# Clustered attention and two expert stages on one core: another order for the first three halves of the attention

## The chip, the cores and the metric

One Trainium2 chip, one of its cores. The metric is the device time in microseconds (us) of one execution. The kernel before took 1049.97 us, the median of three runs (1048.81 to 1053.58). Engines in the rows: PE is TensorE, PEld its weight loads, DVE is VectorE, ACT is ScalarE, POOL is GpSimd, SP is SyncE (SPq its queue of DMA issues).

## The reference

Three parts follow each other. The attention works for each of 2 batches x 8 heads on 768 positions of 64 values; each query and key belongs to the nearest of 16 centroids, and a query sees the keys of its own cluster alone.

```python
q_assign = np.argmax(np.einsum('bhsd,hcd->bhsc', q_n, c_n), axis=-1)
k_assign = np.argmax(np.einsum('bhsd,hcd->bhsc', k_n, c_n), axis=-1)
mask = q_assign[:, :, :, None] == k_assign[:, :, None, :]
scores = np.where(mask, scale * np.matmul(q, k.transpose(0, 1, 3, 2)), -1000000000.0)
attn = np.exp(scores - np.max(scores, axis=-1, keepdims=True))
attn = attn / (np.sum(attn, axis=-1, keepdims=True) + 1e-09)
x = np.matmul(attn, v)                       # then [1536, 512]
g = elu(x @ w_in); x = g @ w_out             # 512 -> 2048 -> 512
for e in range(4):                           # p: domain_probs, rows summing to 1
    out += p[:, e:e + 1] * (np.maximum(x @ w1[e], 0.0) @ w2[e])
```

## The kernel before, in words

Products of full precision are made of single-pass ones: every operand is split into a high and a low part (h and l).

The attention takes the heads in 8 pairs (j). A pair has 12 units of 128 queries (six per head), taken two at a time: a *half* w is two units, six halves to a pair, 48 in all. For each unit the steps are: S (scores, do_S: two products of 384 columns of QA with KA, which hold the parts of q and k, then two of QB with KB), M (row maximum, VectorE), E (exponent and row sum, ScalarE), G and R (reciprocal of the sum), P (scaling, GpSimd). Then for each half: T (three groups of four transposes), C and L (the high and low parts of what was transposed: ScalarE, then VectorE, or both GpSimd for four groups of eighteen), V (products with v), X, Y, Z (out of PSUM and into xT). The cluster mask lies inside the score product: QB's and KB's first 16 rows hold one-hots of the clusters of the queries and of the keys; the keys' are times 2^100, less 2^100, so that a key of another cluster gets a huge negative score.

A pair is prepared beforehand: load (DMA of q, k, v), prep_qk (transposes, then high part on ScalarE and low part on VectorE), prep_stacks (DMAs that put these parts into QA, KA, QB, KB; three of them for each of q or k and head), prep_logits (products with the centroids), prep_argmax (three parts on VectorE: maximum and subtraction, rank by a ramp, one-hot), and the one-hots' way into QB and KB. Later pairs do this inside the halves of the pair ahead of them (Q, by prep()); the first pair does it ahead of everything (lines 510 to 544), with first_onehot (line 294) writing QB and KB directly.

Every engine runs its instructions in the order in which they are written, and the framework adds no order of its own. The order of the halves is a sorted list (line 549): each step has a time AT, half w comes PERIOD = 4.6 later than the one before, and some steps have a SHIFT. Only the order counts, not the times. Ahead of S0, E0 and Q0 of half 0 the list's loop inserts the rest of the argmax, the second head's one-hots, and the query preparation of pair 1. All loads and stack transfers are issued on SyncE's one queue, in order. warm(n) (line 504) makes n transposes of the identity that nobody reads.

The first pair's argmax is made for one group at a time; groups 0 and 1 are the queries of the first and second head, 2 and 3 their keys.

Of the kernel before, what the change touches and what calls it, by code (L numbers as in the profile page):

```python
# [34 lines left out]

POOL_SPLITS = (2, 4, 6, 11)
BIG = float(2.0 ** 100)

# [8 lines left out]
def kernel(  # L47
# [31 lines left out]
    identb = const.tile([128, 128], BF16, name="identb")  # L79
    ramp = const.tile([128, 1, C], F32, name="ramp")  # L80
    cc = const.tile([128, HP, 4 * C], F32R, name="cc")
# [22 lines left out]
    def attention():  # L104
# [145 lines left out]
        def prep_argmax(j, part, g0=0, g1=4):  # L250

            yield
            yield
            n = g1 - g0
            if part == 0 and g0 == 0:
                oh_t[j] = (
                    am_p.tile([128, T, 4, 1], F32, tag="mx", name="mx"),
                    am_p.tile([128, T, 4, C], F32, tag="rk", name="rk"),
                    am_p.tile([128, T, 4, C], BF16, tag="oh", name="oh"),
                )  # L260
            if n == 4:
                L, mx, rk, oh = (x.rearrange("p t g c -> p (t g) c") for x in (L_t[j], *oh_t[j]))
            else:
                L, mx, rk, oh = (x[:, :, g0] for x in (L_t[j], *oh_t[j]))
            top = mx.to_broadcast([128, T * n, C])
            if part == 0:
                dve.tensor_reduce(out=mx, in_=L, axis=AX.X, op=ALU.max)
                eng = dve if j == 0 else pool
                eng.tensor_tensor(out=L, in0=L, in1=top, op=ALU.subtract)
            elif part == 1:  # L270
                dve.scalar_tensor_tensor(
                    out=rk, in0=L, scalar=0.0, in1=ramp.to_broadcast([128, T * n, C]), op0=ALU.is_ge, op1=ALU.mult
                )
                dve.tensor_reduce(out=mx, in_=rk, axis=AX.X, op=ALU.max)
            else:
                dve.tensor_tensor(out=oh, in0=rk, in1=top, op=ALU.is_equal)
# [17 lines left out]
        def first_onehot(r, nm):  # L294

            dst, sc, bi = ((QB[r], 1.0, 0.0), (KB[r], BIG, -BIG))[nm == "k"]
            oh = oh_t[0][2]
            for i in range(2):
                ps = ps_t.tile([C, 3 * 128], BF16, tag="t", name="ohps")
                for t in range(3):  # L300
                    pe.transpose(ps[:, t * 128:(t + 1) * 128], oh[:, 3 * i + t, r + 2 * (nm == "k")], identb)
                o = dst[0:C, i * 384:(i + 1) * 384]
                if i == 0:
                    act.activation(out=o, in_=ps, func=AF.Copy, scale=sc, bias=bi)
                else:
                    dve.tensor_scalar(out=o, in0=ps, scalar1=sc, scalar2=bi, op0=ALU.mult, op1=ALU.add)

# [47 lines left out]

        def do_S(w, i):
            u = HALF * w + i
            j, r, t = u // UP, (u % UP) // T, u % T
            s = (2 * j + r) % NSET
            ps = ps_s.tile([128, 2, 512], F32, tag="s", name="s")  # L360
            c = slice(t * 128, (t + 1) * 128)
            for n in range(2):
                m = slice(384 * n, 384 * n + 384)
                pe.matmul(ps[:, n, 0:384], lhsT=QA[s][:, c], rhs=KA[s][:, m], start=True, stop=False)  # L364
            for n in range(2):
                m = slice(384 * n, 384 * n + 384)
                pe.matmul(ps[:, n, 0:384], lhsT=QB[s][:, c], rhs=KB[s][:, m], start=False, stop=True)  # L367
            s_t[u] = ps

# [134 lines left out]
        def warm(n):  # L504

            ps = ps_t.tile([128, 3, 128], F32, tag="t", name="warm")
            for i in range(n):
                pe.transpose(ps[:, i % 3, :], ident, ident)

# [6 lines left out]
        for c in range(C):  # L516
            dve.memset(ramp[..., c:c + 1], float(C - c))
        for i in range(NSET):
# [15 lines left out]
        run(prep_logits(0, "q", 1))  # L534
        for nm in "qk":
            load(1, nm)
        for nm in "qk":
            prep_stacks(0, nm, 1)
        run(*(prep_logits(0, "k", i) for i in range(2)))
        warm(14)  # L540
        run(*(prep_argmax(0, i, g, g + 1) for i in range(3) for g in (0, 2)))
        first_onehot(0, "k")
        first_onehot(0, "q")
        run(prep_v(0, 0))
# [3 lines left out]

        items = sorted(
            (at + PERIOD * w + SHIFT.get((nm, w % (2 * NH)), 0) + (4 if nm[0] == "Q" and w == 0 else 0), w, nm)  # L550
            for nm, at in AT.items() for w in range(NW)
        )
        for at, w, nm in items:
            if w == 0 and nm == "S0":
                run(*(prep_argmax(0, i, g, g + 1) for i in range(3) for g in (1, 3)))
            if w == 0 and nm == "E0":
                first_onehot(1, "q")
                first_onehot(1, "k")
                oh_t.pop(0)
            if w == 0 and nm == "Q0":  # L560
                run(*(prep_qk(1, "q", i) for i in range(2)))
                prep_stacks(1, "q", 0)
            do[nm[0]](w, int(nm[1:]))
# [491 lines left out]
```

## Time and profile before

| | |
|---|---|
| median of 3 runs | 1049.97 us |
| profiled execution | 1049.63 us, span 1047.9 us |
| busy share of the span | PE 98%, PEld 88%, DVE 70%, ACT 50%, POOL 37% |
| instructions | 16446 |
| attention ends (last product with v, L441) | near 248.7 us |

The profile's first part gives each engine's busy share over the whole span; it mixes the attention, in which all engines work, with the two expert stages behind it, in which TensorE works almost alone. A stage is therefore read from windows: the busy time of each engine in a stretch, beside the clock that TensorE was granted (1.00 is 2.4 GHz, 0.50 is 1.2 GHz). The timeline lists the instructions of an engine with start and length; a bracket behind one names what ended the idle time ahead of it. TensorE's instructions are pipelined, so that a length includes time in which the next one already runs.

### The profile page before, as it was taken

How to read it: one execution, taken by the hardware profiler on the slowest of the kernel's cores; microseconds unless marked ns; L12 is line 12 of the kernel's file. 1: busy time of each engine (PE TensorE's matmuls, PEld its weight loads, DVE VectorE, ACT ScalarE, POOL GpSimd, SP SyncE). 2: the span in 40 equal slices, each digit the busy share in tenths (PEclk: the TensorE clock that was granted, in tenths of full speed). 3: DMA queues.
4: the chain of work that ended last, by engine and by line, in shares of the span. 5: the costliest groups of instructions: out<-in, count | busy, mean ns of one | idle time of the engine just before them, and what ended most of it. 6: DMA issues, size and time to landing. Idle time of an engine off the chain costs nothing.

```text
span 1047.9 us, 16446 instructions
## 1 busy us (share of the span) xinstructions
PE 1029.1 (98%) x6253; PEld 918.4 (88%) x6253; DVE 735.4 (70%) x1248; ACT 524.2 (50%) x1081; POOL 392.8 (37%) x394
## 2 busy tenths in 40 slices
PE   8999999999999999999999999999999999999998
PEld 7989999989877888888888898999999898989897
DVE  6999989998689674326576765666666767666665
ACT  4989999988676563324442332233332333332331
POOL 2888888889578766344641000000000000000000
PEclk8999999999999999999999999999999999999999
DMA  8746664431323221010002101111101111001003
GB/s 184 186 109 155 144 145 104 111 92 33 114 96 122 81 96 66 1 41 0 1 1 81 41 1 41 41 41 41 35 7 41 41 42 41 17 25 41 1 1 121
DMA packets 61790, 67.53 MB, mean 64 GB/s; under 512 B 29008, under 2 KB 47440, under 8 KB 61712
## 3 DMA queue, kind: packets, MB, share of 16 engines
q1 hardware_dynamic: 61712, 66.49, 22.4%
q8 instruction: 49, 0.80, 0.3%
q14 instruction: 29, 0.24, 0.1%
HBM read 43.08 MB, written 3.15 MB: 44 GB/s over the span
## 4 chain that ended last, share of the span: by engine, by line
PE 84%; DVE 8%; ACT 4%; issue 2%; DMA 1%; SPq 1%; POOL 1%; DVEq 0%; ACTq 0%; POOLq 0%
PE a L915 35%; PE h L765 23%; PE h L745 10%; PE x L441 5%; PE tps L412 4%; PE s L364 2%; PE s L367 2%; DVE pl L433 2%; DVE nm L373 1%; PE lps L239 1%; PE lps L240 1%; DVE wa L710 1%; ACT ph L425 1%; PE qkps L199 1%; ACT e L382 1%
## 5 line engine op out<-in xcount | busy, mean ns | idle before, releaser
L765 PEld LDWEIGHTS h<-x,w1op 128*128 128x128 f32 x2016 | 257.4, 190 | 10.3 <-ACT r L776 1.2
L765 PE MATMUL h<-x,w1op 128*128 128x256 f32 x2016 | 261.2, 285 | 1.0 <-ACT r L776 1.0
L915 PE MATMUL a<-w2op,gh 128*128 128x512 f32 x768 | 238.4, 392 | 0.0
L915 PEld LDWEIGHTS a<-w2op,gh 128*128 128x128 f32 x768 | 138.0, 188 | 23.9
L924 DVE SCALAR_TENSOR_TENSOR acc<-a,prob,acc 128x512 f32<-128x512 f32 x180 | 129.7, 746 | 40.2 <-PE a L915 40.2
L915 PE MATMUL a<-w2op,gl 128*128 128x512 f32 x384 | 149.8, 390 | 0.0
L745 PE MATMUL h<-xT,wh 128*128 128x512 f32 x384 | 118.5, 390 | 0.6 <-DVE gg L754 0.5
L400 POOL TENSOR_SCALAR p<-e,sm 128x768 f32<-128x768 f32 x96 | 88.4, 927 | 40.2 <-DVE sm L394 29.0
L754 DVE SCALAR_TENSOR_TENSOR gg<-r,h 128x512 f32<-128x512 f32 x48 | 32.9, 685 | 96.5 <-ACT r L753 75.4
L373 DVE TENSOR_REDUCE nm<-s 128x1 f32<-128x768 f32 x96 | 90.9, 947 | 2.8 <-PE s L367 2.6
L382 ACT ACTIVATE e<-s,nm 128x768 f32<-128x768 f32 x96 | 86.6, 902 | 4.5 <-POOL p L400 2.8
L412 PE MATMUL tps<-ident,p 128*128 128x128 f32 x576 | 83.5, 277 | 2.9 <-DVE pl L433 2.7
L745 PEld LDWEIGHTS h<-xT,wh 128*128 128x128 f32 x384 | 71.9, 188 | 16.2 <-DVE gg L754 1.4
L776 ACT ACTIVATE r<-h 128x256 f32<-128x256 f32 x48 | 18.4, 384 | 134.8 <-PE h L765 134.8
L915 PEld LDWEIGHTS a<-w2op,gl 128*128 128x128 f32 x384 | 72.1, 188 | 15.6
L433 DVE TENSOR_TENSOR pl<-tps,ph 128x512 fp32r<-128x512 f32 x112 | 76.2, 683 | 6.6 <-ACT ph L425 5.2
L441 PE MATMUL x<-ph,v 128*128 128x256 f32 x288 | 76.6, 298 | 1.4 <-DVE xs L461 1.3
L752 ACT ACTIVATE r<-h 128x512 f32<-128x512 f32 x48 | 28.6, 595 | 97.7 <-PE h L745 96.9
L915 PE MATMUL a<-gh,wh 128*128 128x512 f32 x192 | 74.9, 390 | 1.0 <-ACT acc L931 0.9
L755 POOL TENSOR_SCALAR gh<-gg 128x512 fp32r<-128x512 f32 x48 | 41.0, 854 | 92.0 <-DVE gg L754 89.2
L915 PE MATMUL a<-gl,wh 128*128 128x512 f32 x192 | 74.8, 390 | 0.0
L915 PE MATMUL a<-gh,wl 128*128 128x512 f32 x192 | 74.7, 389 | 0.0
(152 smaller groups left out, 1942.1 us busy)
## 6 DMA issues: line engine op xcount, KB each, us to landing
st<-in_moe_w_dram SPq DMA_DIRECT2D x32, 512.0 KB, 4.3
st<-in_moe_w_in_dram SPq DMA_DIRECT2D x14, 512.0 KB, 3.7
st<-in_moe_w_out_dram SPq DMA_DIRECT2D x14, 512.0 KB, 4.6
QA<-qh SPq DMA_DIRECT2D x32, 192.0 KB, 4.2
nq<-in_q_dram SPq DMA_DIRECT2D x16, 192.0 KB, 3.8
nk<-in_k_dram SPq DMA_DIRECT2D x16, 192.0 KB, 3.9
nv<-in_v_dram SPq DMA_DIRECT2D x8, 384.0 KB, 3.9
QB<-ql SPq DMA_DIRECT2D x16, 192.0 KB, 4.2
```

The lines of the kernel that those rows point to most:

```text
L373: dve.tensor_reduce(out=m_t[w][:, i:i + 1], in_=s_t[HALF * w + i][:, :, 0:384], axis=AX.XY, op=ALU.max, negate=True)
L382: act.activation(out=e, in_=s_t.pop(u)[:, :, 0:384], func=AF.Exp, bias=m_t[w][:, i:i + 1], accum_out=e_t[w][0][:, i:i + 1])
L400: pool.tensor_scalar(p, e_t[w][1 + i].rearrange("p a b -> p (a b)"), e_t[w][0][:, i:i + 1], 1.0, ALU.mult, ALU.mult)
L412: pe.transpose(ps[:, x, :], p_t[w][i][:, c * 128:(c + 1) * 128], ident)
L433: dve.tensor_tensor(out=l, in0=ps, in1=h.bitcast(F32), op=ALU.subtract)
L441: pe.matmul(x_t[w], lhsT=v2[j][:, r, c, :], rhs=t[:, :, c, :], start=(c == 0 and t is ph[w]), stop=(c == T - 1 and t is pl[w]),)
L745: pe.matmul(ps, lhsT=w[:, 0, f], rhs=x, start=(kk == 0 and i == 0), stop=(kk == KD - 1 and i == 2))
L754: dve.scalar_tensor_tensor(out=gg, in0=r, scalar=-1.0, in1=ps, op0=ALU.add, op1=ALU.max)
L755: pool.tensor_scalar(gh, gg, 1.0, 0.0, ALU.mult, ALU.add)
L765: pe.matmul(ps, lhsT=w[wz][kk], rhs=x[xz][:, kk], start=(start and kk + i == 0), stop=(stop and kk == 1 and i == 2), skip_group_check=True,)
L915: pe.matmul(ps, lhsT=x, rhs=y, start=(opens and i == 0), stop=(closes and i == len(ops) - 1))
L924: dve.scalar_tensor_tensor(out=t, in0=ps, scalar=pr, in1=t, op0=ALU.mult, op1=ALU.add)
```

## The change

For the first pair, the query clusters of both heads are found first, in one argmax over two groups (ramp is doubled for it), then the first head's keys, then the second head's. A one-hot is transposed into one PSUM tile; queries are copied by ScalarE alone, keys half by ScalarE and half by VectorE. A score can be written in two parts, QA x KA (do_SA) and QB x KB (do_SB); the first two scores have their first parts ahead of the keys' one-hots. The load of the next pair's keys stands behind the second head's stack transfers in place of ahead of them. The identity transposes are 25, 3, 4 and 6 ahead of the list, and four times 4 in it (54 in place of 39), in a PSUM tile of V's pool. Halves 0, 1 and 2 are placed by a start and a pace of their own (0.6, 0.8, 0.9 of AT); W and Q steps keep their places. From the third transpose group of half 4 on, the order of the list is the one of before.

```diff
--- before.py
+++ after.py
@@ -34,6 +34,8 @@
 }
 
 POOL_SPLITS = (2, 4, 6, 11)
+
+WARM = ((2.65, 4), (4.8, 4), (5.6, 4), (6.6, 4))
 BIG = float(2.0 ** 100)
 
 
@@ -77,7 +79,7 @@
     const = ctx.enter_context(tc.tile_pool(name="const", bufs=1))
     ident = const.tile([128, 128], F32, name="ident")
     identb = const.tile([128, 128], BF16, name="identb")
-    ramp = const.tile([128, 1, C], F32, name="ramp")
+    ramp = const.tile([128, 1, 2 * C], F32, name="ramp")
     cc = const.tile([128, HP, 4 * C], F32R, name="cc")
     prob = const.tile([128, B * T, E], F32, name="prob")
 
@@ -260,16 +262,23 @@
                 )
             if n == 4:
                 L, mx, rk, oh = (x.rearrange("p t g c -> p (t g) c") for x in (L_t[j], *oh_t[j]))
+            elif n == 1:
+                L, mx, rk, oh = (x[:, :, g0] for x in (L_t[j], *oh_t[j]))
             else:
-                L, mx, rk, oh = (x[:, :, g0] for x in (L_t[j], *oh_t[j]))
-            top = mx.to_broadcast([128, T * n, C])
+                L, mx, rk, oh = (x[:, :, g0:g1] for x in (L_t[j], *oh_t[j]))
+            shape = [128, T, n, C] if 1 < n < 4 else [128, T * n, C]
+            top = mx.to_broadcast(shape)
             if part == 0:
                 dve.tensor_reduce(out=mx, in_=L, axis=AX.X, op=ALU.max)
                 eng = dve if j == 0 else pool
                 eng.tensor_tensor(out=L, in0=L, in1=top, op=ALU.subtract)
             elif part == 1:
+                both = len(shape) == 4
+                x, y = (z.rearrange("p t g c -> p t (g c)") if both else z for z in (L, rk))
+                order = ramp if both else ramp[..., 0:C]
                 dve.scalar_tensor_tensor(
-                    out=rk, in0=L, scalar=0.0, in1=ramp.to_broadcast([128, T * n, C]), op0=ALU.is_ge, op1=ALU.mult
+                    out=y, in0=x, scalar=0.0, in1=order.to_broadcast([128, x.shape[1], order.shape[2]]),
+                    op0=ALU.is_ge, op1=ALU.mult,
                 )
                 dve.tensor_reduce(out=mx, in_=rk, axis=AX.X, op=ALU.max)
             else:
@@ -295,15 +304,15 @@
 
             dst, sc, bi = ((QB[r], 1.0, 0.0), (KB[r], BIG, -BIG))[nm == "k"]
             oh = oh_t[0][2]
-            for i in range(2):
-                ps = ps_t.tile([C, 3 * 128], BF16, tag="t", name="ohps")
-                for t in range(3):
-                    pe.transpose(ps[:, t * 128:(t + 1) * 128], oh[:, 3 * i + t, r + 2 * (nm == "k")], identb)
-                o = dst[0:C, i * 384:(i + 1) * 384]
-                if i == 0:
-                    act.activation(out=o, in_=ps, func=AF.Copy, scale=sc, bias=bi)
-                else:
-                    dve.tensor_scalar(out=o, in0=ps, scalar1=sc, scalar2=bi, op0=ALU.mult, op1=ALU.add)
+            ps = ps_t.tile([C, S], BF16, tag="t", name="ohps")
+            for t in range(T):
+                pe.transpose(ps[:, t * 128:(t + 1) * 128], oh[:, t, r + 2 * (nm == "k")], identb)
+            if nm == "q":
+                act.activation(out=dst[0:C], in_=ps, func=AF.Copy)
+                return
+            a, b = slice(0, 384), slice(384, 768)
+            act.activation(out=dst[0:C, a], in_=ps[:, a], func=AF.Copy, scale=sc, bias=bi)
+            dve.tensor_scalar(out=dst[0:C, b], in0=ps[:, b], scalar1=sc, scalar2=bi, op0=ALU.mult, op1=ALU.add)
 
         def run(*gens):
             for g in gens:
@@ -354,18 +363,29 @@
         s_t, m_t, e_t, p_t, ph, pl, t_t, x_t, xs_t, q_t = ({} for _ in range(10))
 
         def do_S(w, i):
+            do_SA(w, i)
+            do_SB(w, i)
+
+        def do_SA(w, i):
             u = HALF * w + i
+            if u in s_t:
+                return
             j, r, t = u // UP, (u % UP) // T, u % T
             s = (2 * j + r) % NSET
-            ps = ps_s.tile([128, 2, 512], F32, tag="s", name="s")
+            ps = s_t[u] = ps_s.tile([128, 2, 512], F32, tag="s", name="s")
             c = slice(t * 128, (t + 1) * 128)
             for n in range(2):
                 m = slice(384 * n, 384 * n + 384)
                 pe.matmul(ps[:, n, 0:384], lhsT=QA[s][:, c], rhs=KA[s][:, m], start=True, stop=False)
+
+        def do_SB(w, i):
+            u = HALF * w + i
+            j, r, t = u // UP, (u % UP) // T, u % T
+            s = (2 * j + r) % NSET
+            c = slice(t * 128, (t + 1) * 128)
             for n in range(2):
                 m = slice(384 * n, 384 * n + 384)
-                pe.matmul(ps[:, n, 0:384], lhsT=QB[s][:, c], rhs=KB[s][:, m], start=False, stop=True)
-            s_t[u] = ps
+                pe.matmul(s_t[u][:, n, 0:384], lhsT=QB[s][:, c], rhs=KB[s][:, m], start=False, stop=True)
 
         def do_M(w, i):
             if i == 0:
@@ -503,9 +523,9 @@
 
         def warm(n):
 
-            ps = ps_t.tile([128, 3, 128], F32, tag="t", name="warm")
+            ps = ps_x.tile([128, 2, 128], F32, tag="x", name="warm")
             for i in range(n):
-                pe.transpose(ps[:, i % 3, :], ident, ident)
+                pe.transpose(ps[:, i % 2, :], ident, ident)
 
         c0, cn = load_centroids()
         load(0, "q")
@@ -514,7 +534,7 @@
         pool.tensor_copy(identb, ident)
         warm(25)
         for c in range(C):
-            dve.memset(ramp[..., c:c + 1], float(C - c))
+            dve.memset(ramp[..., c::C], float(C - c))
         for i in range(NSET):
             for t in (QB[i], KB[i]):
                 pool.memset(t[0:32].bitcast(F32), 0.0)
@@ -532,34 +552,54 @@
         run(*(prep_qk(0, "k", i) for i in range(2)))
         prep_stacks(0, "k", 0)
         run(prep_logits(0, "q", 1))
-        for nm in "qk":
-            load(1, nm)
+        load(1, "q")
         for nm in "qk":
             prep_stacks(0, nm, 1)
-        run(*(prep_logits(0, "k", i) for i in range(2)))
-        warm(14)
-        run(*(prep_argmax(0, i, g, g + 1) for i in range(3) for g in (0, 2)))
+        load(1, "k")
+        run(prep_argmax(0, 0, 0, 2))
+        run(prep_logits(0, "k", 0))
+        run(prep_argmax(0, 1, 0, 2), prep_argmax(0, 2, 0, 2))
+        run(prep_logits(0, "k", 1))
+        warm(3)
+        for r in range(2):
+            first_onehot(r, "q")
+        run(*(prep_argmax(0, i, 2, 3) for i in range(3)))
+        for i in range(2):
+            do_SA(0, i)
+        warm(4)
         first_onehot(0, "k")
-        first_onehot(0, "q")
+        run(*(prep_argmax(0, i, 3, 4) for i in range(3)))
+        warm(6)
         run(prep_v(0, 0))
         NW = NPAIR * 2 * NH
         do = dict(S=do_S, M=do_M, E=do_E, G=do_G, R=do_R, P=do_P, T=do_T, C=do_C, L=do_L, V=do_V, X=do_XC, Y=do_XA,
                   Z=do_XS, Q=do_Q, W=do_W)
 
-        items = sorted(
-            (at + PERIOD * w + SHIFT.get((nm, w % (2 * NH)), 0) + (4 if nm[0] == "Q" and w == 0 else 0), w, nm)
-            for nm, at in AT.items() for w in range(NW)
-        )
-        for at, w, nm in items:
-            if w == 0 and nm == "S0":
-                run(*(prep_argmax(0, i, g, g + 1) for i in range(3) for g in (1, 3)))
-            if w == 0 and nm == "E0":
-                first_onehot(1, "q")
+        def place(at, w, nm):
+            if w > 2 or nm[0] in "QW":
+                return at + PERIOD * w + (4 if w == 0 and nm[0] == "Q" else 0)
+            at0, pace = ((1.5, 0.6), (4.6, 0.8), (9.2, 0.9))[w]
+            return at0 + pace * at
+
+        items = [
+            (place(at, w, nm) + SHIFT.get((nm, w % (2 * NH)), 0), w, nm) for nm, at in AT.items() for w in range(NW)
+        ]
+
+        def start(w, i):
+            if i == 0:
                 first_onehot(1, "k")
                 oh_t.pop(0)
-            if w == 0 and nm == "Q0":
-                run(*(prep_qk(1, "q", i) for i in range(2)))
-                prep_stacks(1, "q", 0)
+            elif i < 3:
+                run(prep_qk(1, "q", i - 1))
+                if i == 2:
+                    prep_stacks(1, "q", 0)
+            else:
+                warm(WARM[i - 3][1])
+
+        items += [(at, 0, f"_{i}") for i, at in enumerate((2.6, 2.7, 4.3))]
+        items += [(at, 0, f"_{i + 3}") for i, (at, _) in enumerate(WARM)]
+        do["_"] = start
+        for at, w, nm in sorted(items):
             do[nm[0]](w, int(nm[1:]))
         run(*w_gen)
         actx.close()
```

## Rows read from the trace of the kernel before

**Rows 1.** Windows: length, busy us (instructions) per engine, clock, DMA share, GB/s

```profile
10.00:20.00 10.00, 9.55 (x53) 8.43 (x52) 6.39 (x25) 2.37 (x7) 0.84 (x1) 0.66 1.03 218
20.00:34.00 14.00, 12.48 (x92) 10.90 (x93) 12.77 (x27) 11.67 (x30) 6.97 (x9) 1.00 0.96 221
34.00:50.00 16.00, 15.49 (x123) 14.75 (x122) 15.12 (x26) 15.06 (x36) 14.21 (x17) 1.00 0.72 178
60.00:80.00 20.00, 19.02 (x146) 17.78 (x146) 18.87 (x35) 18.02 (x42) 18.88 (x22) 1.00 0.44 107
```

**Rows 2.** Granted TensorE clock where it fell and rose, same columns

```profile
11.60:11.70 0.10, 0.10 (x3) 0.10 (x2) 0.00 (x0) 0.00 (x0) 0.00 (x0) 0.50 0.56 123
18.40:18.50 0.10, 0.10 (x2) 0.10 (x2) 0.07 (x2) 0.00 (x0) 0.00 (x0) 0.87 1.51 313
```

**Rows 3.** Identity transposes (warm): ns min/median/max, first and last start

```profile
L508 PE MATMUL warm<-ident x7: 421/421/421, 3.1 to 4.4; 128*128 128x128 f32 x7
...
L508 PE MATMUL warm<-ident x11: 272/273/273, 4.8 to 5.9; 128*128 128x128 f32 x11
...
L508 PE MATMUL warm<-ident x14: 421/421/474, 12.9 to 15.7; 128*128 128x128 f32 x14
```

**Rows 4.** Timeline of TensorE: start, length (us), engine, line, operation

```profile
12.92 3.25 PE L508 MATMUL warm<-ident 128*128 128x128 f32 x14
16.10 1.60 PE L301 MATMUL ohps<-identb,oh 128*16 128x128 bf16 x12
17.63 0.97 PE L364 MATMUL s<-KA,QA 128*128 128x384 f32 x2
18.43 0.52 PE L367 MATMUL s<-KB,QB 96*128 96x384 f32 x2
...
20.32 0.67 PE L301 MATMUL ohps<-identb,oh 128*16 128x128 bf16 x9 [0.67 <-DVE oh L276]
...
24.34 0.30 PE L239 MATMUL lps<-cc,qh 128*128 128x64 f32 x1
...
25.03 0.60 PE L364 MATMUL s<-KA,QA 128*128 128x384 f32 x2
```

**Rows 5.** Timeline of VectorE, same columns

```profile
11.25 0.25 DVE L245 TENSOR_TENSOR L<-lps,ltmp 128x96 f32<-128x96 f32 x1
...
13.58 0.24 DVE L267 TENSOR_REDUCE mx<-L 128x6 f32<-128x96 f32 x1
...
15.40 0.42 DVE L276 TENSOR_TENSOR oh<-rk,mx 128x96 bf16<-128x96 f32 x2
17.02 0.55 DVE L306 TENSOR_SCALAR KB<-ohps 16x384 fp32r<-16x384 bf16 x1 [1.21 <-PE ohps L301]
...
20.35 0.95 DVE L373 TENSOR_REDUCE nm<-s 128x1 f32<-128x768 f32 x1
...
24.21 0.95 DVE L373 TENSOR_REDUCE nm<-s 128x1 f32<-128x768 f32 x1
...
29.68 0.69 DVE L433 TENSOR_TENSOR pl<-tps,ph 128x512 fp32r<-128x512 f32 x1 [0.52 <-ACT ph L425]
```

**Rows 6.** Timeline of ScalarE, same columns

```profile
16.69 0.48 ACT L304 ACTIVATE KB<-ohps 16x384 fp32r<-16x384 bf16 x1 [3.32 <-PE ohps L301]
...
21.51 0.88 ACT L382 ACTIVATE e<-s,nm 128x768 f32<-128x768 f32 x1
...
24.92 0.87 ACT L201 ACTIVATE kh<-qkps 128x384 fp32r<-128x384 f32 x2 [0.68 <-DMA KB<-kh]
```

**Rows 7.** Timeline of GpSimd, same columns

```profile
26.64 1.80 POOL L400 TENSOR_SCALAR p<-e,sm 128x768 f32<-128x768 f32 x2 [15.80 <-DVE sm L394]
```

**Rows 8.** Timeline of SyncE's DMA queue, same columns

```profile
14.89 1.29 SPq L146 DMA_DIRECT2D nk<-in_k_dram  x2
...
20.23 1.47 SPq L228 DMA_DIRECT2D KB<-kh  x1
```

**Rows 9.** One DMA issue: KB each, us to landing

```profile
KB<-kh SPq DMA_DIRECT2D x1, 192.0 KB, 4.6
```

## The prediction

> **What bounds the kernel now.** I read the windows by stage first. From 34 to 80 us TensorE is busy 15.49 of 16 and 19.02 of 20 us, and VectorE 15.12 and 18.87 [rows 1]: two engines in lockstep, each with 5% or less to spare, so a lag carried into this stretch can shrink by little and leaves with the rest of the program, whose instruction order from the fifth half of the attention on (its third transpose group) is the same in both kernels. What can change is therefore the start, before some 34 us. There the reader sees VectorE busy 6.39 of 10 us (10 to 20 us) and 12.77 of 14 (20 to 34), and a TensorE clock of 0.66 on average between 10 and 20 us [rows 1]: it falls to 0.50 (1.2 GHz) at 11.6 us, after a run of small logits matmuls with gaps, and is back at 2.4 GHz from 18.45 [rows 2]. Identity transposes are 421 ns long at the low level and 272 at the full one [rows 3]; their spacing is 3.18 / 14 = 0.227 us low [rows 4] and 1.1 / 10 = 0.11 full [rows 3].
>
> Third, the timelines, which give the chain that starts the attention: last logits sum, argmax of two cluster groups on VectorE (13.58 to 15.82), one-hot transposes (16.10), copies (from 16.69), first scores (17.63), the argmax of the two other groups, and the first row maximum M at 20.35 [rows 4 to 6]. From that M on VectorE hardly rests.
>
> **The change part by part.** All times are on the profiled execution's clock: span 1047.9 us, 1049.63 with the 1.73 us around it; the median of the runs is 0.34 above.
>
> *Argmax of the queries together, before the keys.* The query logits are summed by 11.50 [rows 5]. VectorE's step takes 0.25 us for 96 elements and 0.69 for 512 [rows 5], so one of 192 lies between; on the line through both it is 0.35. Five such and the first key half's logits sum (0.25): 11.50 + 1.75 + 0.25 = 13.5 us for both heads' query clusters, 2.3 us sooner than before.
>
> *TensorE from there, at the low clock.* Its work up to 12.92 is as before, so the clock should fall at the same place. Three warm transposes take 0.68 (13.60), twelve query one-hot transposes 1.60 [rows 4] (15.20), the first parts of two scores 2 x 0.80 (17.63 to 18.43 is one) (16.80), four transposes 0.91 (17.70), six key one-hots 0.80 (18.50). The copies KB end 0.60 later (0.55 each, side by side on ScalarE and VectorE) [rows 5, 6]: 19.10. The query copies go to ScalarE whole: between 0.48 and 0.96, I take 0.9, hidden under 16.8 to 18.5. VectorE's argmax of key group 2 (five steps of 0.25 and a gap, 13.58 + 5 x 0.27 = 14.95 [rows 5]) is hidden too. The argmax of group 3 is queued behind the KB copy: 19.10 + 1.35 = 20.45. M follows at 20.5: **+0.15** against 20.35. The second parts of the scores, behind six more transposes, are done near 20.3, in its shadow. Splitting a score costs nothing else: nothing else wants its two buffers then. The sooner queries win nothing, because keys still stand behind them.
>
> *What follows M.* One copy of a query one-hot leaves VectorE after M: **-0.5** (0.55 less overlap). But the order now lets the two engines wait on each other. ScalarE: exponent of unit 0 (until 22.35), KB half (22.8), query half qh (23.2). VectorE: M to 21.45, KB half to 21.95, then ql, which needs qh, and behind it in the queue M of unit 1, whose scores are long there: VectorE stands from 21.95 to 23.25, **1.3**. M then ends at 24.65, the exponent at 25.55, the second qh at 25.95: VectorE stands from 24.65 to 26.0, **1.35**. The next M (third score) starts at 26.45; before it started at 24.21 [rows 5, 6].
>
> *The reordered load.* SyncE's queue issues the next keys at 14.89; now six stack transfers go first, which puts the issue where the last of those was, 20.23 [rows 8], landing 4.6 us on [rows 9]: 24.8. The DMA engines are at 1.03 and 0.96 of capacity with 218 and 221 GB/s [rows 1], so the last of the same sixteen transfers lands when it did. What goes is ScalarE's wait of 0.68 for KB<-kh at 24.92 [rows 6]; what is late next are these keys. TensorE's transposes of them stand ahead of the third score in its queue, and TensorE has nothing from about 22.1 (second query half) to 24.85. The third score then runs at 25.2 to 26.0, just within VectorE's wait for ql: no further term while that cover lasts; without it the wait alone puts the third M at 26.05 instead of 24.21.
>
> *First transposes ahead of the fifth score's M.* The fourth M starts near 28.4. Then TensorE has four warm transposes, logits (24.34 to 25.03, 0.69) [rows 4], four more, the fifth score (two rows like that of 25.03, overlapping: 0.8) and only then the transposes of half 0, done at 31.3; POOL's p is ready sooner (27.5 + 0.9 [rows 7]). ScalarE's copy of 512 elements takes between 0.48 (384) and 0.88 (768) [rows 6], I take 0.6; VectorE's pl follows at 31.9, before the fifth M in the queue. VectorE stands idle from 29.3, less one logits sum of 0.25: **2.35**. Before, pl came at 29.68 [rows 5], but with the fifth M already done.
>
> *More warm transposes*: 54 for 39, in all 15 more, but eleven fewer ahead of the first one-hots; the twelve behind the third score take 12 x 0.11 = 1.3 us of TensorE, which are in the times above.
>
> A rule against the change: the Trainium skill (TensorE: Matmul & The Clock Gate, Part 4: PE-mode transpose) says that transposes do not count as activity that brings the full clock. In the trace they did: with nothing but transposes on TensorE they went from 421 to 272 ns near 4.8 us [rows 3]. But 14 others ran through at 421. By the rule the low clock would last on past 18.45; by the rows it ends as before, which is what I sum with. The rule's own time stands under the rivals.
>
> **Sum.** +0.15 - 0.5 + (1.3 + 1.35 + 2.35 = 5.0) - 1.23 (the waits VectorE had from 20 to 34 us, 14.00 - 12.77 [rows 1], which these replace) = +3.4 at 34 us. In 34 to 50 and 60 to 80 VectorE had 0.88 + 1.13 = 2.0 us idle; with transposes and products of the first halves already done sooner in its order I let half of that be regained: -1.0. Total +2.4: 1049.63 + 2.4 = **1052.0 us**.
>
> **Rivals.**
> *Faster, the waits hidden.* If the clock is back when the first scores start (15.2), their parts take 0.8, the warm transposes 0.44, the one-hots 0.45 [rows 3, 4]: KB at 17.5, argmax at 18.85, M at 18.9, 1.45 us sooner. If besides the two engines don't wait on each other, -1.45 - 0.5 - 1.23 = -3.2: 1046.4. For it: query one-hots and dense scores now fill the stretch where 14 transposes were. Against: keys land at 24.8 whatever the clock, and the queues' orders are plain.
>
> *Nothing.* The 3.4 us are made good by 80 us, or the waits are half as long as I read: 1049.6, plus or minus 1. For it: engines with slack of 5% over 46 us have 2.3 us to give. Against: VectorE and TensorE wait for each other there.
>
> *Clearly slower: the clock falls again.* TensorE idles from 22.1 to 24.85 behind the keys. If the clock falls on that and stays low as long as it did before (11.6 to 18.45, 6.85 us [rows 2]), half of 6.85 is lost where nothing is to spare: 1049.6 + 3.4 + 3.4 = 1056.4. It decides if the granted clock shows 0.50 again between 22 and 32 us. For it: the clock fell at 11.6 although TensorE was busy 9.55 of the 10 us from 10 to 20 [rows 1]. Against: transposes stand on both sides of the gap.
>
> *Transposes that don't hold the clock* (the rule above). The low clock past 18.45: six transposes 1.36 and the score's second part to 20.8, M at 20.85 instead of 20.5: 1052.4. The first 25 transposes of the trace speak against it.
>
> **How the numbers follow.** Forecast 0.45 (1050.5 to 1054), faster with hidden waits 0.27 (1045.5 to 1048.5), nothing 0.13, clock falls 0.10 (1054.5 to 1058), transposes that don't count 0.05. A measurement here can tell 0.5%, 5.2 us, from no change: faster means under 1044.7, slower over 1055.2. No case reaches the first but the tail of the second, 0.03; slower takes most of the clock case and a tail of the forecast, 0.09; the rest, 0.88, is within. Range 1046 to 1056: it reaches to the means of both outer cases, and takes in the logits and argmax bounds (0.25 to 0.69 a step, five steps, at most 1.7 us).
>
> **What would show it.** Right: the clock row falls at 11.6 and rises near 18.4; M near 20.5; the third M near 26.4; VectorE's waits before ql on ScalarE; TensorE idle ahead of the transposes of the next keys, released by a DMA; VectorE idle from 20 to 34 us about 5 us. Wrong: the third M at or before 24.2, or a clock that is back by 15 us, or a VectorE that from 34 to 80 us shows under half its 2.0 us of idle time. The forecast fails if the first three halves' transposes, done sooner, let TensorE reach the common order earlier than before.

## The result, and the profile after

The changed kernel takes 1066.55 us (median of 6 runs, 1063.95 to 1068.71) against 1051.59 for the kernel before: ratio 1.0144, 95% interval 1.0118 to 1.0169. That is 15 us slower, clearly, where 1052.0 and no more than 1056 were forecast. The kernel before varies more than its first three runs showed (1048.81 to 1056.35 over all comparisons), so each ratio below is to its runs beside the kernel told of, on the same chip. Three of the six runs behind 1051.59 are among its quickest (1048.81 to 1049.97), and its medians in the later comparisons are 1053.59 to 1054.47. Against those the loss is 12 to 13 us, so a difference of a few thousandths between 1.0144 and a ratio below is less than it looks. Disturbed executions are left out; for e4 and e5 the profiled one was among them, so that no profile of theirs is used.

All of it is in the attention's start. The row maximum of the first unit of a half starts as follows (us, from the timelines of VectorE):

| half | 0 | 1 | 2 | 3 | 4 | 5 | 6 | 47 |
|---|---|---|---|---|---|---|---|---|
| before | 20.35 | 24.21 | 27.97 | 32.08 | 36.60 | 41.48 | 46.66 | 256.12 |
| after | 19.48 | 26.63 | 37.16 | 44.84 | 50.22 | 57.22 | 64.21 | 274.12 |
| lag | -0.9 | +2.4 | +9.2 | +12.8 | +13.6 | +15.7 | +17.6 | +18.0 |

The lag is made in halves 1 to 6 and then carried to the end nearly unchanged (17.6 and 18.0). It is 18 us and not 15, since the two profiled executions took 1067.57 and 1049.63 us. The windows that answer to those of before [rows 1]:

```profile
10.00:20.00 10.00, 7.79 (x66) 6.18 (x64) 6.80 (x23) 3.59 (x8) 0.69 (x1) 1.00 0.99 217
20.00:34.00 14.00, 9.99 (x54) 9.60 (x52) 6.03 (x11) 5.19 (x13) 1.79 (x2) 0.73 0.89 196
34.00:50.00 16.00, 12.66 (x76) 10.39 (x74) 8.72 (x17) 9.75 (x23) 8.96 (x11) 0.91 0.36 86
60.00:80.00 20.00, 18.58 (x140) 17.45 (x139) 17.40 (x32) 15.96 (x39) 13.14 (x18) 0.98 0.63 148
```

VectorE is busy 6.03 and 8.72 us in the second and third row; before it was 12.77 and 15.12. TensorE's clock is 1.00 from 10 to 20 us, where it had been 0.66, but 0.73 from 20 to 34: it falls later. Near the fall and the rise:

```profile
26.00:27.00 1.00, 1.00 (x8) 0.96 (x7) 0.37 (x1) 0.51 (x2) 0.00 (x0) 0.79 0.71 151
27.00:36.00 9.00, 9.00 (x40) 8.81 (x39) 2.80 (x6) 1.89 (x5) 1.79 (x2) 0.50 0.91 202
36.00:37.00 1.00, 0.73 (x5) 0.33 (x4) 0.61 (x2) 1.00 (x3) 0.00 (x0) 0.59 0.00 0
```

Nine whole microseconds at 1.2 GHz and a part of two more (0.42 and 0.82 by the means): 10.2 us, in the middle of the halves and not ahead of them as before [rows 2]. A second stretch of 3.4 us follows between 57 and 61 us, 0.50 at its bottom:

```profile
57.00:58.00 1.00, 1.00 (x6) 0.86 (x6) 1.00 (x2) 1.00 (x3) 0.00 (x0) 0.65 0.00 0
...
60.00:61.00 1.00, 1.00 (x8) 1.00 (x7) 0.91 (x2) 0.76 (x2) 0.78 (x2) 0.65 0.46 86
```

TensorE's timeline shows what went before the first:

```profile
20.55 0.82 PE L201 MATMUL qkps<-ident,nq 128*128 128x128 f32 x6
25.37 0.52 PE L201 MATMUL qkps<-ident,nk 128*128 128x128 f32 x3 [4.01 <-DMA nk<-in_k_dram]
...
26.43 0.92 PE L528 MATMUL warm<-ident 128*128 128x128 f32 x4
...
30.35 1.05 PE L528 MATMUL warm<-ident 128*128 128x128 f32 x4
...
33.10 0.99 PE L379 MATMUL s<-KA,QA 128*128 128x384 f32 x2
...
34.53 1.91 PE L432 MATMUL tps<-ident,p 128*128 128x128 f32 x8
...
40.78 0.39 PE L461 MATMUL x<-ph,v 128*128 128x256 f32 x1 [0.70 <-POOL ph L450]
42.12 0.39 PE L461 MATMUL x<-pl,v 128*128 128x256 f32 x1 [0.96 <-POOL pl L451]
...
43.86 0.59 PE L379 MATMUL s<-KA,QA 128*128 128x384 f32 x2
```

The next pair's keys arrive 4.01 us after TensorE was ready for them (I had 2.75). The clock then falls within 1.3 us, and from there everything up to the transposes of 34.53 runs at the low clock: the two score products at 33.10 take 0.99 us, the two at 43.86, at the full clock, 0.59. At 40.78 and 42.12 TensorE stands again, now for GpSimd. VectorE's timeline:

```profile
19.48 0.95 DVE L393 TENSOR_REDUCE nm<-s 128x1 f32<-128x768 f32 x1
21.85 0.54 DVE L315 TENSOR_SCALAR KB<-ohps 16x384 fp32r<-16x384 bf16 x1 [1.42 <-ACT KB L314]
...
25.16 0.56 DVE L205 SCALAR_TENSOR_TENSOR ql<-qkps,qh 128x384 fp32r<-128x384 f32 x1 [1.44 <-ACT qh L203]
26.63 0.96 DVE L393 TENSOR_REDUCE nm<-s 128x1 f32<-128x768 f32 x1 [0.91 <-PE s L388]
...
36.39 0.26 DVE L247 TENSOR_TENSOR L<-lps,ltmp 128x96 f32<-128x96 f32 x1 [4.68 <-ACT ltmp L245]
36.56 0.68 DVE L453 TENSOR_TENSOR pl<-tps,ph 128x512 fp32r<-128x512 f32 x1
37.16 0.95 DVE L393 TENSOR_REDUCE nm<-s 128x1 f32<-128x768 f32 x1
...
44.12 0.42 DVE L481 TENSOR_TENSOR xs<-x,xt 64x256 f32<-64x256 f32 x1 [4.02 <-ACT xt L473]
44.84 0.96 DVE L393 TENSOR_REDUCE nm<-s 128x1 f32<-128x768 f32 x1 [0.31 <-PE s L388]
...
54.06 0.42 DVE L481 TENSOR_TENSOR xs<-x,xt 64x256 f32<-64x256 f32 x1 [2.35 <-ACT xt L473]
...
62.98 0.42 DVE L481 TENSOR_TENSOR xs<-x,xt 64x256 f32<-64x256 f32 x1 [2.07 <-ACT xt L473]
```

There are three stretches. First come waits of 1.42 and 1.44 us for ScalarE (forecast 1.3 and 1.35), with 0.91 us more for the third score, which stands behind the late keys in TensorE's queue. Then come 4.68 us until ScalarE has copied the first transposes and, behind them in its queue, the part ltmp of the next pair's logits:

```profile
35.62 0.60 ACT L445 ACTIVATE ph<-tps 128x512 fp32r<-128x512 f32 x1 [6.08 <-PE tps L432]
36.11 0.24 ACT L245 ACTIVATE ltmp<-lps 128x96 f32<-128x96 f32 x1
```

Last come 4.02 us ahead of Y (xs), behind which the fourth half's row maximum (44.84) stands in the queue; ahead of the next two Y it is 2.35 and 2.07 us again, and the lag grows on. The wait at 44.12 leads to GpSimd:

```profile
38.35 1.79 POOL L420 TENSOR_SCALAR p<-e,sm 128x768 f32<-128x768 f32 x2 [8.79 <-DVE sm L414]
40.10 0.62 POOL L450 TENSOR_SCALAR ph<-raw 128x512 fp32r<-128x512 f32 x1
40.81 1.26 POOL L451 TENSOR_TENSOR pl<-raw,ph 128x512 fp32r<-128x512 f32 x1
```

GpSimd scales half 1 first (1.79 us), because that stands first in its queue, then splits the third group of half 0 (0.62 and 1.26). The product with v of half 0 needs that split, and in TensorE's queue it stands ahead of the score of half 3 (43.86).

### The profile page after: what moved, and what is told of

Same layout as the page of the kernel before. It is cut to its first block, busy times and chain, and to the rows that moved or that the text cites. A ratio compares the mean times of both kernels' runs of the same rounds, so it can differ in the third digit from the quotient of the medians.

```text
span 1065.6 us, 16458 instructions
## 1 busy us (share of the span) xinstructions
PE 1036.0 (97%) x6268; PEld 923.3 (87%) x6268; DVE 734.7 (69%) x1241; ACT 525.3 (49%) x1081; POOL 393.0 (37%) x394
## 4 chain that ended last, share of the span: by engine, by line
PE 81%; DVE 7%; POOL 4%; ACT 4%; issue 2%; DMA 1%; SPq 0%; DVEq 0%; POOLq 0%; ACTq 0%
PE a L955 35%; PE h L805 23%; PE h L785 10%; PE x L461 4%; PE tps L432 3%; POOL p L420 2%; PE s L379 2%; PE s L388 2%; DVE pl L453 1%; DVE nm L393 1%; ACT ph L445 1%; PE warm L528 1%; PE qkps L201 1%; DVE wa L750 1%; POOL xT L493 1%
## 5 line engine op out<-in xcount | busy, mean ns | idle before, releaser
L794 DVE SCALAR_TENSOR_TENSOR gg<-r,h 128x512 f32<-128x512 f32 x48 | 32.9, 685 | 96.5 <-ACT r L793 75.0
L432 PEld LDWEIGHTS tps<-ident,p 128*128 128x128 f32 x576 | 65.9, 142 | 10.4 <-DVE pl L453 4.8
```

Source lines behind the costliest of these rows:

```text
L432: pe.transpose(ps[:, x, :], p_t[w][i][:, c * 128:(c + 1) * 128], ident)
L794: dve.scalar_tensor_tensor(out=gg, in0=r, scalar=-1.0, in1=ps, op0=ALU.add, op1=ALU.max)
```

## The experiments

Compared are ratios to the kernel before; the changed kernel has 1.0144. "Theory" and "rival" are those of the expectation that stands above each result.

**e1, keys first.** The next pair's keys loaded ahead of the stacks.

```diff
-        load(1, "q")
+        for nm in "qk":
+            load(1, nm)
         for nm in "qk":
             prep_stacks(0, nm, 1)
-        load(1, "k")
```

> The changed kernel with one part undone: the load of the next pair's keys stands ahead of the second head's stack transfers again, as before the change. Theory (keys and order): the changed kernel is some 15 us slower because TensorE stands 4.0 us for these keys and then runs 9.6 us (26.8 to 36.4) at the low clock, and because the compressed order of the first three halves makes VectorE and TensorE wait for GpSimd afterwards. Then this kernel gets back the 4.0 us, and 4.8 us for half of 9.6: some 1058 us, and the granted clock stays at 1.00 from 20 to 36 us. Rival (the order alone): the wait was covered by the waits between VectorE and ScalarE, and the time stays within 2 us of 1066.5.

1065.22 us, ratio 1.011 (1.0086 to 1.0133). There is no wait for the keys, yet the fifth unit's maximum starts at 37.20 as in the changed kernel (37.16), and the clock is at 0.50 from 28.3 to 45.3 us. (This was the longest of the four executions, 1068.44; the others took 1063.85 to 1066.46.) The rival comes nearer: the late load alone is not it, and the low clock comes without it.

**e2, the old order of the halves,** keys still late.

```diff
-            if w > 2 or nm[0] in "QW":
+            if True:
```

> The changed kernel with one part undone: all halves of the attention are placed as before the change (no pace of their own for the first three), the late load of the keys stays. Theory (keys and order): the wait for the keys and the low clock stay, what the order cost behind them goes (the lag grew from 9.2 us at the third half's row maximum to some 17 at the seventh's): some 1059 us. Rival (keys alone): the order is harmless once the clock is up, and the time stays above 1064.

1053.56 us, ratio 1.0015 (0.9995 to 1.0035). More than the theory gave it: nine tenths of the loss are gone by ratio, 13.0 us by the medians, with a wait of 2.1 us for the keys still in the trace and no low clock behind it.

**e3, the clock held** by 36 transposes in the wait.

```diff
                 if i == 2:
                     prep_stacks(1, "q", 0)
+                    warm(36)
```

> The changed kernel with 36 more identity transposes behind the second half of the next pair's queries, where TensorE waits for the keys (about 4 us of work at 0.11 us each, inside the wait of 4.0 us). It tells the wait from the clock. Theory: the wait stays, the clock stays at 1.00 through 27 to 36 us, and half of the 9.6 us at the low clock comes back: some 1062 us. Rival (the wait itself does the harm, TensorE's clock is covered by other engines): within 2 us of 1066.5. Second rival (transposes do not count for the clock): the clock falls near 27 us all the same.

1063.67 us, ratio 1.0096 (1.0078 to 1.0114). The windows of the transposes and of what was low before:

```profile
22.80:26.80 4.00, 4.00 (x39) 4.00 (x38) 1.90 (x4) 2.37 (x7) 0.00 (x0) 1.00 0.43 96
27.00:36.00 9.00, 8.32 (x66) 7.80 (x63) 5.86 (x13) 5.30 (x15) 2.31 (x3) 1.00 0.93 209
```

The clock is at 1.00 from 20.2 us until it falls at 40.6, for 3.4 us:

```profile
40.00:41.00 1.00, 1.00 (x9) 1.00 (x9) 0.00 (x0) 0.70 (x2) 0.80 (x1) 0.82 0.00 0
...
44.00:45.00 1.00, 0.70 (x4) 0.38 (x2) 1.00 (x3) 0.92 (x3) 0.76 (x1) 0.97 1.03 246
```

What the low clock was worth is told only roughly: 5 us by the ratios (1.0144 less 1.0096), 3 by the medians. Two executions of the changed kernel with the same mean clock as e3's four (0.995) took 1063.95 and 1064.88, hardly more than e3's 1063.30 to 1065.43. Most of the loss is there with the clock held. Its chain of waits between the row maxima of halves 2 and 3 (start, us, what):

```profile
35.26 0.08 DVE sm L414
...
35.50 1.79 POOL p L420 x2
37.29 0.60 POOL ph L450
...
37.96 1.27 POOL pl L451
...
39.27 0.39 PE x L461
...
41.71 0.64 PE s L379 x2
...
43.03 0.96 DVE nm L393
```

Scaling, split, product, score, maximum: one engine after another, at full clock up to the product (39.27); the score behind it runs at the low one.

**e4, keys first and the old order** (both edits above).

> The changed kernel with both undone: keys loaded ahead of the second head's stacks, and all halves placed as before the change. What is left is the joint argmax of the queries, the one-hots in one piece, the first scores in two parts and the identity transposes. Theory (keys and order are all of it): 1048.5 to 1052 us, as before the change, perhaps 1 us under it since the first row maximum comes 0.9 us sooner. Rival (the waits between ScalarE and VectorE around the next pair's query preparation, or the 15 more transposes, cost by themselves): 1054 or more.

1051.77 us, ratio 0.9985 (0.9973 to 0.9997): with what is left of the change the kernel is about 1.6 us quicker on the mean. At the same clock it is not: e4's eight executions with a mean granted clock of 0.996 or more took 1051.14 to 1052.27 us, four such of the kernel before beside them 1049.53 to 1050.56. But of e4's executions only one had a lower clock (0.994, 1053.83), of the kernel before's 14 (0.992 to 0.995, 1053.10 to 1055.21). The late keys cost 2 us (medians) to 3 (ratios) under the old order, e2 against e4; the two intervals touch.

**e5, products late**, and **e6, transposes and products late**, in halves 0 to 2.

```diff
-            if w > 2 or nm[0] in "QW":
+            if w > 2 or nm[0] in "QWVXYZ":     # e5
+            if w > 2 or nm[0] in "QWTCLVXYZ":  # e6
```

> The changed kernel, but in the first three halves the products with v and what follows them (steps V, X, Y, Z) keep the places of before; all other steps stay compressed. With the old order of all steps the kernel took 1053.6 us, so the compressed order costs 13. Theory (the chain through GpSimd): with V, X and Y early, the product of the first half stands in TensorE's queue behind GpSimd's splits, and the fourth half's first row maximum stands in VectorE's queue behind Y: 4.0 us of VectorE idle from 40.1 to 44.1, and once more a half later. Then some 6 of the 13 us come back: 1060. Rival (the transposes do the harm): no change, over 1064.

> The changed kernel, but in the first three halves all steps from the transposes on (T, C, L and V, X, Y, Z) keep the places of before; only scores, maxima, exponents, reciprocals and scaling stay compressed. Theory (transposes and products pulled ahead of the next halves' scores make every engine wait on the slowest): nearly all of the 13 us come back, 1053 to 1056. Rival (the order of maxima and exponents among the preparation does it): 1060 or more.

e5: 1060.53 us, ratio 1.0052 (1.0033 to 1.0071), as expected. e6: 1059.11 us, ratio 1.0044 (1.0023 to 1.0064): between theory and rival, and as a whole not told apart from e5. Among the executions with a mean clock of 0.995 or more, four of each, e6 took 1055.75 to 1056.59 and e5 1057.60 to 1058.77, so the transposes' places are worth some 2 us there. Something else of the compressed order is left: e6's five executions at 0.992 or less took 1061.62 to 1063.98.

**e7, half 0 alone compressed.**

```diff
-            if w > 2 or nm[0] in "QW":
+            if w > 0 or nm[0] in "QW":
```

> The changed kernel, but only the first half has a start and pace of its own; halves 1 and 2 stand as before the change. If the harm is the first half's transposes and products being ahead of the scores of halves 2 and 3 (theory), most of it stays: 1060 or more. If it comes from the three compressed halves running into each other (rival), it falls to 1057 or less.

1056.56 us, ratio 1.003 (1.0016 to 1.0044): the rival. The harm grows with the number of halves that run into each other.

**e8, no transposes in the list** (WARM empty).

> The changed kernel without the four groups of four identity transposes within the list of halves. In the profile 12 of them run at the low clock between 26 and 33 us, some 0.25 us each, ahead of scores. Theory: they cost up to 3 us of TensorE there, and they do not hold the clock: 1063 to 1065. Rival (they keep the low clock shorter): 1068 or more.

1067.73 us, ratio 1.012 (1.0105 to 1.0135): not told apart from the changed kernel. The clock is at 0.50 all the way from 24.2 to 44.6 us, against 10.2 us with them, and the time is not longer. That engines that wait in turn cover much of a low clock is a reading that no run here tests.

**e9, queries later,** and **e10, the same without the list's transposes,** on e4.

```diff
-        items += [(at, 0, f"_{i}") for i, at in enumerate((2.6, 2.7, 4.3))]
+        items += [(at, 0, f"_{i}") for i, at in enumerate((2.6, 4.25, 4.3))]
```

> The changed kernel with the keys loaded ahead of the stacks and all halves placed as before (together 1051.8 us), and besides the next pair's first half of queries prepared behind the second unit's row maximum, together with the second half, not between the two maxima. Theory (VectorE and ScalarE wait for each other there, 1.3 and 1.35 us in the forecast, 1.42 and 1.44 in the changed kernel's trace): 1 to 2.5 us less, 1049.3 to 1050.8, and under the kernel before. Rival (these waits are covered by TensorE's and GpSimd's): no change, 1051.3 to 1052.3.

> The same without the 16 identity transposes in the list of halves. Theory (TensorE is not the bound of that stretch, but 12 of the transposes stand ahead of scores): up to 1 us less than with them, if the clock holds without them. Rival (they hold the clock): the clock falls between 20 and 30 us and the time is 1 us or more longer than with them.

e9: 1051.92 us, ratio 0.9984 (0.9973 to 0.9996), no gain over e4. The edit had little to take away: of the two waits for ScalarE the second, ahead of ql, is not in e2's trace either, which has the old order and the first plan, and the first, 1.42 us, is still in e9's. e10: 1053.70, ratio 0.9993 (0.9978 to 1.0008). The intervals overlap, but the rival's sign is there: in e10's profile the clock is low from 29.8 to 36.6 us, where in e9's it stays at 1.00, and four of e10's twelve executions have a mean clock of 0.990 or less (1056.09 to 1057.35 us), none of e9's nine.

**e11, the kernel before with the changed places of halves 0 to 2 alone.**

```diff
-            (at + PERIOD * w + SHIFT.get(...) + (4 if nm[0] == "Q" and w == 0 else 0), w, nm)
+            ((at + PERIOD * w + (4 if nm[0] == "Q" and w == 0 else 0) if w > 2 or nm[0] in "QW"
+              else (1.5, 4.6, 9.2)[w] + (0.6, 0.8, 0.9)[w] * at) + SHIFT.get(...), w, nm)
```

> The kernel before with one part of the change alone: the first three halves have the start and pace of the changed kernel; argmax, one-hots, loads and identity transposes stay as before. Theory (the order alone does it): 8 to 14 us slower than the kernel before, 1061 to 1067. Rival (the order does harm only behind the late keys or the moved preparation): within 4 us of the kernel before.

1063.16 us, ratio 1.0077 (1.0064 to 1.009): the theory. VectorE:

```profile
30.54 0.26 DVE L245 TENSOR_TENSOR L<-lps,ltmp 128x96 f32<-128x96 f32 x1 [2.48 <-ACT ltmp L243]
...
31.31 0.95 DVE L373 TENSOR_REDUCE nm<-s 128x1 f32<-128x768 f32 x1
...
38.27 0.42 DVE L461 TENSOR_TENSOR xs<-x,xt 64x256 f32<-64x256 f32 x1 [4.03 <-ACT xt L453]
39.01 0.96 DVE L373 TENSOR_REDUCE nm<-s 128x1 f32<-128x768 f32 x1 [0.32 <-PE s L367]
```

The same two waits, 2.48 and 4.03 us, without late keys. The clock is low from 27.5 to 30.9 us, which takes in the first, and at 1.00 during the second: the order alone makes them.

**e12, no splits on GpSimd in halves 0 and 1.**

```diff
-        if 3 * (w % (2 * NH)) + g in POOL_SPLITS:      # in do_C and do_L
+        if w > 1 and 3 * (w % (2 * NH)) + g in POOL_SPLITS:
```

> The changed kernel, but the two transpose groups of halves 0 and 1 that GpSimd splits are split by ScalarE and VectorE, so that no product of these halves waits for GpSimd's splits (0.62 and 1.26 us each, queued behind the scaling of the next half). Theory (the early products stand in TensorE's queue behind GpSimd): VectorE's wait of 4.0 us at 40 us and TensorE's of 2.1 and 1.1 us go for the most part, some 4 us in all: 1061 to 1064. Rival (the products wait for the scaling itself or for something else): above 1065.

1059.70 us, ratio 1.0047 (1.0032 to 1.0062): more came back than expected, 7 us by the medians and 10 by ratio. Its profiled execution also had no low clock between 20 and 60 us, so the fairer neighbour is e3, and to that it is 4 us by the medians, 5 by ratio. TensorE no longer waits for GpSimd's splits. Left over are a wait for the keys (TensorE), VectorE's for Y (3.1 in three) and the first transposes, and the two for ScalarE of 1.4 us each (columns: total us, times, longest):

```profile
PE qkps L201 <- DMA nk<-in_k_dram: 3.4, 1, 3.4
```

```profile
DVE xs L481 <- ACT xt L473: 3.1, 3, 1.5
DVE L L247 <- ACT ltmp L245: 2.3, 1, 2.3
```

**e13, e12 with keys first,** and **e14, e6 with keys first.**

> The changed kernel without GpSimd's splits in halves 0 and 1 (that alone: ratio 1.0047 to the kernel before, some 5 us slower), and with the keys loaded ahead of the stacks. In the former's trace TensorE still stands 3.4 us for the keys. Theory (what is left is that wait, and the transposes ahead of the fifth score, VectorE's wait of 2.3 us): ratio 1.001 to 1.003. Rival (the wait for the keys is covered by the transposes' chain): ratio 1.004 or more.

> The changed kernel with the keys loaded ahead of the stacks, and the transposes, splits and products of the first three halves at the places of before; scores, maxima, exponents and scaling stay compressed. With late keys this had a ratio of 1.0044. Theory (early transposes, early products and late keys are all of it): ratio 0.998 to 1.002, as with the old order of all steps (0.9985). Rival (the compressed scores, maxima and exponents cost by themselves): ratio 1.003 or more.

e13: 1060.09 us, ratio 1.0063 (1.0048 to 1.0078): the rival; nothing came back for the keys' wait. VectorE's wait for the first transposes is 3.8 us in place of 2.3, at a clock that is low from 29.4 to 32.9. e14: 1058.96 us, ratio 1.0055 (1.0039 to 1.0072): the rival too. Compressed scores, maxima, exponents and scaling leave the kernel some 5 us behind the one before; the profiled execution, at a mean clock of 0.997, took 1056.43, the three at 0.992 took 1058.68 to 1060.57. VectorE in e14:

```profile
23.63 0.55 DVE L315 TENSOR_SCALAR KB<-ohps 16x384 fp32r<-16x384 bf16 x1 [1.42 <-ACT KB L314]
...
26.94 0.56 DVE L205 SCALAR_TENSOR_TENSOR ql<-qkps,qh 128x384 fp32r<-128x384 f32 x1 [1.44 <-ACT qh L203]
...
40.92 0.56 DVE L279 SCALAR_TENSOR_TENSOR rk<-L,ramp 128x384 f32<-128x384 f32 x1 [1.93 <-POOL L L274]
```

The waits for ScalarE stand there again, and at 40.92 one of 1.93 us for GpSimd, whose queue now has the scaling of half 2's first unit ahead of a split and of the next pair's subtraction. Which of these, or the clock, makes the 5 us was not tried.

## Why the prediction was wrong

*Where the change acts, and what becomes of a lag.* Right: the lag of half 6 is the lag of the last half, and nothing behind the start moved.

*To the third row maximum: the number is right, and in part by luck.* +2.24 forecast, +2.4 measured. The waits for ScalarE came as forecast (1.42 and 1.44 us for 1.3 and 1.35). But in this execution the clock did not fall at 11.6, so that the first maximum came 0.9 us sooner, not 0.15 later, and the 0.91 us for the third score, forecast at nothing, made up for that. In e2, e3 and e7, whose instructions up to there are the same, the clock fell at 13.1 to 13.4 and the first maximum came at 20.97 to 21.14.

*"Just within VectorE's wait for ql: no further term while that cover lasts."* The cover was too short for VectorE (0.91 us, and 0.64 in e3) and did not reach TensorE's clock. The wait was 4.01 us, the clock fell, and the rival "the clock falls again" took place: with the clock held (e3) 3 to 5 us are gone. Its price of 3.4 was of the right size, its chance of 0.10 was not. That the wait made the clock fall is not shown: it falls at 28.3 us in e1, which has no such wait, and not in e2, which has one of 2.1 us.

*"First transposes ahead of the fifth score's M": right at the full clock.* Forecast 2.35 us of VectorE; 2.30 with the clock held (e3), 2.48 in e11, 4.68 at the low clock. From the first maximum to the fifth the working gives 12.1 us (20.5 to 32.6, which is pl at 31.9 and its 0.69); it was 13.2 in e3 and 17.7 in the changed kernel's profile.

*The step that failed is the last of the sum: "I let half of that be regained: -1.0", on +3.4 at 34 us.* I walked through the queues to the fifth row maximum and took the rest as a balanced stretch that gives something back. The compressed order had more waits there: early products that TensorE keeps ahead of the scores while GpSimd still scales the next half, and Y ahead of a row maximum in VectorE's queue. The lag after half 2 grew by 8.4 us (9.2 to 17.6); I had -1.0. From the first row maximum of half 2 to that of half 6 it takes, in the profiles (us):

| before | changed | e3, clock held | e11, order alone | e12, no splits | e2, old order |
|---|---|---|---|---|---|
| 18.7 | 27.1 | 26.6 | 27.0 | 21.8 | 18.7 |

So the order alone makes the whole of this growth, and some 5 of the 8 us go with GpSimd's splits in two halves. (Each of the three at 27 us has 3.4 us of low clock in that stretch, e12 and e2 have none; by an estimate from the two levels that is at most half of 3.4, 1.7 us, of the difference.) In the times of the whole kernel: order alone 1.0077 (e11), old order 1.0015 (e2). What makes the other 3 us is not shown.

*The reordered load* was sized rightly (24.8 us, and TensorE took the keys at 25.37), but it is not an independent term: 2 to 3 us under the old order (e2 against e4), 1 to 3 in the changed kernel (e1, intervals overlap), nothing beside the split-free halves (e13).

*The merged argmax, the whole one-hots, the split scores and the added identity transposes* gain about 1.6 us together on the mean (e4), by more executions at the high clock and not by shorter work at the same clock. The Trainium skill's rule on transposes (TensorE: Matmul & The Clock Gate, Part 4: PE-mode transpose) does not hold here: in e3 TensorE ran nothing but transposes for 4 us and the clock stayed at 1.00.

The faster kernel the experiments point to is e4, or e9, all of the change but its order and its load: ratios 0.9985 (0.9973 to 0.9997) and 0.9984 (0.9973 to 0.9996) to the kernel before. That is a gain on the mean alone: the quickest executions of the kernel before (1049.53 and 1050.10 beside them) were quicker than any of either.

## What to carry to other kernels

When an edit moves steps forward in queues that run in order, walk each queue until every step that moved has run, not until the first engines look busy: a step pulled ahead of its inputs holds all that stands behind it, and the lag was not given back in the 200 us that followed here. Name for each moved step the slowest engine that feeds it; here that was GpSimd, which TensorE's busy share never shows. Price a wait on TensorE with its clock, also where another engine's wait covers it. And look at the clock of every execution before comparing kernels: a gain of 1.6 us on the mean went here with how often the clock stayed up.

## What the hardware showed that was not expected

The time of the clock's first fall differs between executions with the same instructions up to there: not before 26.6 us in the changed kernel's profile, near 13 in e2 and e3. With it go the times: one kernel's executions fall into groups by the mean granted clock. Of the kernel before, beside the experiments, six at 0.996 or more took 1049.53 to 1050.58 us and 63 at 0.995 or less 1052.75 to 1056.35. Of e6, five at 0.994 or more took 1055.75 to 1056.59 and five at 0.992 or less 1061.62 to 1063.98. What lets the clock fall in one execution and not in the next stays open.

A low clock of 20.4 us (e8) cost no more than one of 10.2 us (the changed kernel), with 3.4 us more after 50 us in both. Both lay among waits of other engines; whether that is the reason was not tried.
